# A 64-row tile with both parts side by side, and a reordered passage into the last stage

## The chip, the cores and the metric

The kernel runs on one core of one Trainium2 chip. The metric is the device time of one execution in microseconds (us). Engines are named as in the profile: PE is TensorE's matmul and PEld its weight load, DVE is VectorE, ACT is ScalarE, POOL is GpSimd, SP is the engine whose queue issues most transfers. Times in the text are counted from the start of the span.

## What is computed

Three layers follow one another, in fp32: attention with 8 global and 96 local columns, a layer of 8 experts of which each row uses one, and a channel mix with a shift by one row. The change touches the second and the third.

```python
def _moe_ref(x, w_gate, w_local, w1, w2):
    ...                                  # x: 2 x 768 rows of 512; each row has one expert e
            h = np.maximum(x[b, s] @ w1[e], 0.0)          # w1[e]: 512 x 1024
            out[b, s] = p[e] * (h @ w2[e])                # w2[e]: 1024 x 512

def _moe2_ref(x, mu_k, mu_r, w_k, w_v, w_r):
    x_prev = ...                         # x moved by one row
    xk = mu_k * x + (1.0 - mu_k) * x_prev
    xr = mu_r * x + (1.0 - mu_r) * x_prev
    k = np.maximum(xk @ w_k, 0.0)
    v = k * k @ w_v
    r = 1.0 / (1.0 + np.exp(-(xr @ w_r)))
    return (r * v).astype(np.float32)
```

## The kernel before

Each fp32 operand of a product is split into a high part (type fp32r, written by ScalarE with an activation Copy) and a low part (the difference, written by VectorE). A product is three matmuls into one PSUM bank: high by high, high by low, low by high (`mm3`, L631 to L634). Every engine works through its own queue in the order in which the program emits the instructions; inside `tc.manual_schedule()` (L1580) that order is written out by hand.

The experts are sorted by their number of rows and worked on by rank r = 0 to 7, in tiles of 128 rows. Rank 2 (`THIRD`) has a third tile of `LAST` = 64 rows. Its hidden values are split in `l1m` (L1313) into two tiles `h3h` and `h3l` of 8 chunks by 64 columns. In the second layer `l2_mm` (L659) runs 8 steps of `mm3` per tile, 512 columns wide; the stationary operand is the hidden chunk, 128 columns for a full tile and 64 for the third. `y_out` (L725) copies the bank to SBUF on ScalarE and stores it to `ys` through ScalarE's queue. Ranks 3 and 5 (`SHORT`) go through `short_expert` (L673): one tile surely, a second one under a branch (`tc.If`, L686) that this input skips. TensorE, ScalarE and VectorE all pass that branch, which stands between steps u=7 and u=8; the second turn of the tile (`turn_a(1)`) follows at u=9. Rank 7 runs two tiles through `xs_tile` (L708), 16 steps u each: 8 of the first layer, 8 of the second, turns of the hidden values in between (`hn` to `ehh`, `ehl`).

Weights are prepared ahead of use by `W_` (L1612): each call takes steps off the list `sq`. For an expert's chunk of 1024 columns these are two high halves on ScalarE and one whole low part (`w_lo_all`, L625) on VectorE; the latter also issues the next loads. For the last stage's matrices, called expert `E`, a chunk has four steps: two high halves, two low halves (for chunks 4 to 7 the second high half is on VectorE). They come in the order `WORD` = 8, 9 (w_r), 0 to 3 (w_k), 4 to 7 (w_v). `WS`, `W0` and `W7` say how many steps are taken at each step u. High and low parts live in 9 buffers each; a new chunk waits for the oldest one's last matmul. One chunk of the last stage, (E,7), instead takes two of the six `wraw` buffers that hold raw weights. The matrices of the last stage arrive as fp64 words and are decoded by three VectorE instructions per piece; `B_` (L1353) takes one such instruction at a time, and pieces are loaded through POOL's queue.

The last stage (`stage3`, L1528) works on strips b = 0 to 5 of 256 rows. A strip is gathered from `ys` by POOL, scaled by VectorE, turned by TensorE (`turn`, L1379), copied by ScalarE, mixed in two halves (`mix_a` multiplies by mu on POOL, `mix_b` adds the shifted row on VectorE), and split by `mix_hi` and `mix_lo`. Then come two `r_unit`s of 12 matmuls with a sigmoid each, eight `k_step`s of 12 matmuls of 256 columns (each followed by a ReLU and a squaring, and one step later by a split `k_split`), and two `v_unit`s of 24 matmuls. For strip 0 the r_units come ahead of the k_steps, and gathering, scaling, turning, mixing and splitting are spread by `early` over the steps u of rank 7's second tile, at the places `EARLY_AT` (u from 16 on lies in `stage3`). Strip 1 is prepared between the k_steps of strip 0, one step of the list `a` after each.

Of the kernel before, what the change touches and what calls it, by code (L numbers as in the profile page):

```python
# [16 lines left out]
P = 128  # L17
# [33 lines left out]
EARLY_AT = (7, 9, 8, 11, 12, 12, 12, 11, 12, 13, 13, 13, 13, 14, 16, 18, 16, 18)  # L51
# [517 lines left out]
def build(ctx, tc, ins, out):  # L569
# [40 lines left out]
    def w_hi1(r, c, s):  # L610
        if s == 0:
            last = (r, c) == (E, 7)
            whl[r, c] = tuple(wp.tile([P, 1024], F32R, tag="wraw" if last else f"w{x}", bufs=6 if last else 9, name=f"w{x}{r}_{c}")
                              for x in ("hi", "lo"))
# [44 lines left out]
    def l2_mm(r, ps, i, hs, m=P):  # L659
        ts_ = slice(i * P, i * P + m)  # L660
        for f in range(KF):
# [3 lines left out]
            mm3(ps[0:m, :], hh[:, ts_], hl[:, ts_], wh[:, ds_], wl[:, ds_], f == 0, f == KF - 1)  # L665
            yield f
# [58 lines left out]
    def y_out(pool, ps, row, m=P):  # L725
        yo = pool.tile([P, D], F32, tag="yo", bufs=2, name=f"yo{row}")
        nc.scalar.activation(out=yo[0:m, :], in_=ps[0:m, :], func=ACTF.Copy)  # L727
        nc.scalar.dma_start(out=ys[row:row + m, :], in_=yo[0:m, :])

# [583 lines left out]
    def l1m(r, f):  # L1313
        if r == THIRD and f == 0:
            h3["hl"] = [htile(c, f"h3{c}").rearrange("p (f c) -> p f c", f=KF) for c in "hl"]
# [15 lines left out]
        if not both:  # L1331
            relu_split(hh, hl, ps[:, 0:2 * P])
            relu_split(h3["hl"][0][:, f, :], h3["hl"][1][:, f, :], ps[:, 2 * P:N])
# [60 lines left out]
    def mix_a(b, w, a, z):  # L1394
# [5 lines left out]
        for kk in range(KD):  # L1400
            nc.gpsimd.tensor_scalar(xmix[b, w][:, kk, a:z], strips[b][:, kk, a + 1:z + 1], mu[w][:, 0, kk:kk + 1], 1.0,
                                    op0=ALU.mult, op1=ALU.mult)
# [109 lines left out]
    for u, o in zip(EARLY_AT, (("scale", 0), ("turn", 0), ("scale", 1), ("ra", 0), ("rb", 0), ("hi", 0), ("lo", 0), ("turn", 1), ("ra", 1), ("rb", 1),  # L1512
                              ("hi", 1), ("lo", 1), ("ka", 0), ("kb", 0), ("khi", 0), ("klo", 0), ("khi", 2), ("klo", 2))):
# [14 lines left out]
    def stage3():  # L1528
        small = small_words()
        for b in range(NB):  # L1530
            a, l = prep(b + 1) if b + 1 < NB else ([], [])
            if b == 0:
                gather(2)
                gather(3)
                for f in (KF + KF, KF + KF + 1):
                    early(f)
                W_(2)
                for i in range(2):
                    r_unit(b, i)
                    early(KF + KF + 2 + i)  # L1540
                    W_(5)
            for f in range(KF):
# [5 lines left out]
                if a:  # L1548
# [9 lines left out]
            k_split(b, KF - 1)  # L1558
            if b:
# [13 lines left out]
    WS = (2, 1, 2, 1, 2, 1, 2, 1) + (2, 2, 2, 2, 1, 1, 1, 1)  # L1573
# [4 lines left out]
    W7 = ((1, 0, 0, 0, 2, 1, 2, 0, 1, 2, 2, 1, 1, 0, 0, 0), (0, 0, 0, 0, 0, 2, 2, 2, 2, 0, 2, 0, 0, 0, 0, 2))  # L1578

    with tc.manual_schedule():  # L1580
# [55 lines left out]
        for r in range(1, E - 1):  # L1636
# [27 lines left out]
            for i in range(nt):  # L1664
                ps = n.bank("O", 2)
                m = nrow(r, i)
                if i == 2:
                    src, a = [tuple(h[:, f, 0:m] for h in h3["hl"]) for f in range(KF)], 0
                else:
                    src, a = [hs[r, f] for f in range(KF)], i  # L1670
                for f in l2_mm(r, ps, a, src, m):
# [245 lines left out]
```

## Time and profile before

| | us |
|---|---|
| median of 3 runs (lowest to highest) | 499.07 (498.08 to 499.48) |
| the profiled execution | 497.32 |
| its span, first to last instruction | 495.5 |
| TensorE busy in it (matmuls) | 474.6 |
| VectorE busy | 343.2 |
| ScalarE busy | 261.1 |
| POOL busy | 121.8 |

The busy time of matmuls counts pipelined instructions with modelled ends, so the distance from one start to the next says more than a duration. A row of a timeline gives the start, the time, the engine and line, the operation with the tiles that it writes and reads, and in brackets how long the engine was idle before and what ended that. All rows are of one execution.

### The profile page before, as it was taken

To read this page: it belongs to the slowest core of one execution; us is meant where nothing else is said; L and a number is where in the kernel's file an instruction comes from. 1 tells how busy PE (TensorE), PEld (TensorE's weight loads), DVE (VectorE), ACT (ScalarE), POOL (GpSimd) and SP (SyncE) were. 2 spreads that over 40 slices of the span, in tenths; PEclk is the share of its full clock that TensorE was granted. 3 is DMA by queue.
4 is the path that set the end of the run, shared out by engine and by line. 5 is a ranking of instruction groups with operands and counts; after the bars stand their busy time and mean duration, and the time that the engine had idled before them with its cause. 6 is when DMAs were issued, how large, how long until landed. Compare 5 with 4: busy or idle time off the path is not lost. (4 is left out here: it accounts for less than half of the span.)

```text
span 495.5 us, 9267 instructions
## 1 busy us (share of the span) xinstructions
PE 474.6 (96%) x3231; PEld 408.6 (82%) x3231; DVE 343.2 (69%) x889; ACT 261.1 (53%) x631; POOL 121.8 (25%) x209
## 2 busy tenths in 40 slices
PE   6999999899999999999999999999999999999994
PEld 3789888787788989768878888687989889898984
DVE  6877797796947867958878974897676948264301
ACT  4977876973326744566667655573432504243220
POOL 4111202202200000000000001825482918353220
PEclk9999999989999999999999999989999999999999
DMA  8997576784685886789699832201745533200001
GB/s 159 264 249 159 147 166 181 214 270 137 228 275 182 318 283 227 258 320 336 198 344 321 272 129 65 63 2 63 261 145 184 198 122 134 65 21 13 31 3 48
DMA packets 77128, 87.42 MB, mean 176 GB/s; under 512 B 50961, under 2 KB 51217, under 8 KB 77073
## 3 DMA queue, kind: packets, MB, share of 16 engines
q1 hardware_dynamic: 68304, 63.28, 42.0%
q0 software_dynamic: 4800, 16.78, 10.3%
q10 hardware_dynamic: 3968, 6.69, 3.6%
q8 instruction: 28, 0.46, 0.4%
q14 instruction: 28, 0.22, 0.1%
HBM read 73.75 MB, written 12.98 MB: 175 GB/s over the span
## 5 line engine op out<-in xcount | busy, mean ns | idle before, releaser
L616 ACT ACTIVATE whi<-wraw 128x512 fp32r<-128x512 f32 x128 | 72.2, 623 | 7.6 <-ACT yo L727 3.2
L625 DVE TENSOR_TENSOR wlo<-wraw,whi 128x1024 fp32r<-128x1024 f32 x55 | 66.1, 1218 | 2.1 <-ACT whi L616 2.1
L1438 ACT ACTIVATE sq<-S 128x256 f32<-128x256 f32 x48 | 18.5, 384 | 76.2 <-PE S L634 76.1
L632 PE MATMUL S<-xkh,whi 128*128 128x256 f32 x192 | 55.0, 287 | 0.7 <-ACT whi L616 0.7
L633 PE MATMUL S<-xkl,whi 128*128 128x256 f32 x192 | 53.9, 281 | 0.7 <-DVE xkl L1416 0.7
L634 PE MATMUL S<-xkh,wlo 128*128 128x256 f32 x192 | 54.0, 281 | 0.1
L1448 POOL TENSOR_TENSOR kl<-sq,kh 128x256 fp32r<-128x256 f32 x40 | 35.9, 906 | 69.6 <-issue 36.9
L1478 DVE TENSOR_TENSOR o<-O,sig 128x512 f32<-128x512 f32 (+1 forms) x13 | 8.5, 650 | 52.8 <-PE O L634 33.2
L634 PE MATMUL O<-whi,kl 128*128 128x512 f32 (+1 forms) x104 | 39.2, 377 | 0.6 <-DVE kl L1448 0.6
L633 PE MATMUL O<-wlo,kh 128*128 128x512 f32 (+1 forms) x104 | 39.0, 375 | 0.0
L632 PE MATMUL O<-whi,kh 128*128 128x512 f32 (+1 forms) x104 | 38.7, 372 | 0.0
L633 PEld LDWEIGHTS S<-xkl,whi 128*128 128x128 f32 x192 | 36.9, 192 | 1.3 <-DVE xkl L1416 1.0
L632 PEld LDWEIGHTS S<-xkh,whi 128*128 128x128 f32 x192 | 36.7, 191 | 1.3 <-ACT whi L616 0.9
L634 PEld LDWEIGHTS S<-xkh,wlo 128*128 128x128 f32 x192 | 36.7, 191 | 0.6 <-DVE wlo L621 0.6
L1439 DVE SCALAR_TENSOR_TENSOR sq<-S,sq 128x256 f32<-128x256 f32 x48 | 20.1, 420 | 15.2 <-ACT sq L1438 14.9
L277 POOL DMA_INDIRECT xs<-X,posi x12 | 13.2, 1101 | 52.9 <-DVE acc L295 19.5
L1447 ACT ACTIVATE kh<-sq 128x256 fp32r<-128x256 f32 x48 | 19.7, 412 | 12.2 <-DVE sq L1439 12.2
L634 PE MATMUL O<-whi,hl 128*128 128x512 f32 x64 | 25.1, 393 | 0.0
L633 PE MATMUL O<-wlo,hh 128*128 128x512 f32 x64 | 25.1, 392 | 0.0
L632 PE MATMUL O<-whi,hh 128*128 128x512 f32 x64 | 25.0, 391 | 0.0
L869 ACT ACTIVATE zbig<-zbig,nm 128x232 f32<-128x232 f32 (+1 forms) x48 | 22.4, 466 | 3.3 <-DVE nm L857 3.3
L634 PEld LDWEIGHTS O<-whi,kl 128*128 128x128 f32 x104 | 19.6, 188 | 4.4 <-DVE kl L1448 1.0
(433 smaller groups left out, 1418.6 us busy)
## 6 DMA issues: line engine op xcount, KB each, us to landing
wraw<-in_moe_w_dram SPq DMA_DIRECT2D x64, 512.0 KB, 5.9
dwt<-in_moe_w_v_dram POOLq DMA_DIRECT2D x8, 512.0 KB, 4.7
z<-in_moe_w_k_dram SPq DMA_DIRECT2D x8, 512.0 KB, 5.6
z<-in_moe_w_v_dram SPq DMA_DIRECT2D x8, 512.0 KB, 4.6
ys<-yo ACTq DMA_DIRECT2D x15, 256.0 KB, 5.5
xn<-xs SPq DMA_DIRECT2D x14, 256.0 KB, 4.4
vn<-in_v_dram SPq DMA_DIRECT2D x12, 256.0 KB, 4.2
dwt<-in_moe_w_k_dram POOLq DMA_DIRECT2D x6, 512.0 KB, 6.6
```

Source lines behind the costliest of these rows:

```text
L277: self.nc.gpsimd.indirect_dma_start(self.xs, bass.IndirectOffsetOnAxis(ap=self.posi[:, t:t + 1], axis=0), X[t], None)
L616: nc.scalar.activation(out=whl[r, c][0][:, sl], in_=raws[r, c][:, sl], func=ACTF.Copy)
L625: nc.vector.tensor_tensor(lo, raws.pop((r, c)), hi.bitcast(F32), op=ALU.subtract)
L632: nc.tensor.matmul(out_, lhsT=ah, rhs=bh, start=first, stop=False)
L633: nc.tensor.matmul(out_, lhsT=ah, rhs=bl, start=False, stop=False)
L634: nc.tensor.matmul(out_, lhsT=al, rhs=bh, start=False, stop=last)
L869: nc.scalar.activation(out=pe, in_=pe, func=ACTF.Exp, scale=-1.0, bias=nm[:, h:h + 1], accum_out=sm[:, h:h + 1])
L1438: nc.scalar.activation(out=sq_, in_=ps[:, 0:TB], func=ACTF.Relu)
L1439: nc.vector.scalar_tensor_tensor(sq_, ps[:, 0:TB], 0.0, sq_, op0=ALU.max, op1=ALU.mult)
L1447: nc.scalar.activation(out=hh, in_=sq_, func=ACTF.Copy)
L1448: (nc.gpsimd if b else nc.vector).tensor_tensor(hl, sq_, hh.bitcast(F32), op=ALU.subtract)
L1478: nc.vector.tensor_tensor(o[:, a:z], ps[:, 0:z - a], sig[b, i][:, a:z], op=ALU.mult)
```

## The change

- The third tile of rank 2: high and low hidden values stand side by side, 64 and 64 columns, in two tiles of four chunks (`h3["t"]`). `l2_both` runs two matmuls per chunk, with the high and the low weights, so that the bank's rows 0 to 63 hold the products of the high parts and rows 64 to 127 those of the low parts. `y_both` copies rows 64 to 127 on ScalarE, adds rows 0 to 63 on VectorE and stores through POOL's queue. The product of the two low parts is now included.
- No word is decoded in that tile; in rank 7 words are decoded only at u = 11 to 15 of the first tile.
- (E,9) instead of (E,7) takes the `wraw` buffers; `W7` splits (E,9) in the first tile of rank 7, and `stage3` takes 2 + 3 + 3 steps ahead of the k_steps instead of 2 + 5 + 5.
- One step of `WS` moves from u=6 to u=12.
- Strip 0's `mix_a` runs on ScalarE (activation Copy with a column as scale); `EARLY_AT` ends at u=15, and the second turn and the k mix come earlier in the order.
- A sigmoid of 8 values ahead of rank 7.
- In strip 0 the last step of the list `a` (`mix_b` of strip 1's r) comes after the last `k_split`.

```diff
--- before.py
+++ after.py
@@ -48,7 +48,7 @@
 NTAB = (5, 4)
 X1_AT = (5, 7)
 WNEXT = (1,) * 12 + (0,) * 4
-EARLY_AT = (7, 9, 8, 11, 12, 12, 12, 11, 12, 13, 13, 13, 13, 14, 16, 18, 16, 18)
+EARLY_AT = (7, 9, 9, 10, 10, 11, 11, 11, 12, 12, 12, 13, 13, 13, 15, 15, 15, 15)
 
 
 class Net:
@@ -609,7 +609,7 @@
 
     def w_hi1(r, c, s):
         if s == 0:
-            last = (r, c) == (E, 7)
+            last = (r, c) == (E, WORD[1])
             whl[r, c] = tuple(wp.tile([P, 1024], F32R, tag="wraw" if last else f"w{x}", bufs=6 if last else 9, name=f"w{x}{r}_{c}")
                               for x in ("hi", "lo"))
         sl = slice(s * 512, s * 512 + 512)
@@ -663,6 +663,14 @@
             ds_ = slice((f % 2) * 512, (f % 2) * 512 + 512)
             hh, hl = hs[f]
             mm3(ps[0:m, :], hh[:, ts_], hl[:, ts_], wh[:, ds_], wl[:, ds_], f == 0, f == KF - 1)
+            yield f
+
+    def l2_both(r, ps, ts_):
+        for f in range(KF):
+            ds_ = slice((f % 2) * 512, (f % 2) * 512 + 512)
+            for j, w in enumerate(whl[r, 4 + f // 2]):
+                nc.tensor.matmul(ps, lhsT=ts_[f // 4][:, f % 4].rearrange("p s c -> p (s c)"), rhs=w[:, ds_],
+                                 start=f + j == 0, stop=f == KF - 1 and j == 1)
             yield f
 
     TB = 2 * P
@@ -726,6 +734,12 @@
         yo = pool.tile([P, D], F32, tag="yo", bufs=2, name=f"yo{row}")
         nc.scalar.activation(out=yo[0:m, :], in_=ps[0:m, :], func=ACTF.Copy)
         nc.scalar.dma_start(out=ys[row:row + m, :], in_=yo[0:m, :])
+
+    def y_both(pool, ps, row, m):
+        yo = pool.tile([P, D], F32, tag="yo", bufs=2, name=f"yo{row}")
+        nc.scalar.activation(out=yo[0:m, :], in_=ps[m:2 * m, :], func=ACTF.Copy)
+        nc.vector.tensor_tensor(yo[0:m, :], ps[0:m, :], yo[0:m, :], op=ALU.add)
+        nc.gpsimd.dma_start(out=ys[row:row + m, :], in_=yo[0:m, :])
 
     zp0 = wstack.enter_context(tc.tile_pool(name="zp0", bufs=1))
     w3 = {nm: ins[nm].bitcast(U32) for nm in ("w_k", "w_v", "w_r")}
@@ -1312,7 +1326,7 @@
 
     def l1m(r, f):
         if r == THIRD and f == 0:
-            h3["hl"] = [htile(c, f"h3{c}").rearrange("p (f c) -> p f c", f=KF) for c in "hl"]
+            h3["t"] = [htile(c, f"h3{c}").rearrange("p (f s c) -> p f s c", f=KF // 2, s=2) for c in "hl"]
         N = xhl[r][0].shape[2]
         both = N <= 2 * P
         odd = f % 2
@@ -1330,7 +1344,8 @@
         hs[r, f] = (hh, hl)
         if not both:
             relu_split(hh, hl, ps[:, 0:2 * P])
-            relu_split(h3["hl"][0][:, f, :], h3["hl"][1][:, f, :], ps[:, 2 * P:N])
+            t3 = h3["t"][f // 4][:, f % 4]
+            relu_split(t3[:, 0, :], t3[:, 1, :], ps[:, 2 * P:N])
         elif odd:
             relu_split(*pair["h"], pair["ps"])
 
@@ -1398,8 +1413,11 @@
             else:
                 xmix[b, w] = zp0.tile([P, KD, TB], F32, tag="z0", bufs=2, name=f"xm{w}{b}")
         for kk in range(KD):
-            nc.gpsimd.tensor_scalar(xmix[b, w][:, kk, a:z], strips[b][:, kk, a + 1:z + 1], mu[w][:, 0, kk:kk + 1], 1.0,
-                                    op0=ALU.mult, op1=ALU.mult)
+            o, x, m = xmix[b, w][:, kk, a:z], strips[b][:, kk, a + 1:z + 1], mu[w][:, 0, kk:kk + 1]
+            if b:
+                nc.gpsimd.tensor_scalar(o, x, m, 1.0, op0=ALU.mult, op1=ALU.mult)
+            else:
+                nc.scalar.activation(out=o, in_=x, func=ACTF.Copy, scale=m)
 
     def mix_b(b, w, a, z):
         for kk in range(KD):
@@ -1509,8 +1527,8 @@
                 mix_lo(0, "k", 0, TB, i, i + 2)
 
     EARLY = {}
-    for u, o in zip(EARLY_AT, (("scale", 0), ("turn", 0), ("scale", 1), ("ra", 0), ("rb", 0), ("hi", 0), ("lo", 0), ("turn", 1), ("ra", 1), ("rb", 1),
-                              ("hi", 1), ("lo", 1), ("ka", 0), ("kb", 0), ("khi", 0), ("klo", 0), ("khi", 2), ("klo", 2))):
+    for u, o in zip(EARLY_AT, (("scale", 0), ("turn", 0), ("scale", 1), ("ra", 0), ("rb", 0), ("turn", 1), ("hi", 0), ("lo", 0), ("ra", 1), ("rb", 1),
+                              ("ka", 0), ("hi", 1), ("lo", 1), ("kb", 0), ("khi", 0), ("klo", 0), ("khi", 2), ("klo", 2))):
         EARLY.setdefault(u, []).append(o)
 
     def small_words():
@@ -1532,20 +1550,17 @@
             if b == 0:
                 gather(2)
                 gather(3)
-                for f in (KF + KF, KF + KF + 1):
-                    early(f)
                 W_(2)
                 for i in range(2):
                     r_unit(b, i)
-                    early(KF + KF + 2 + i)
-                    W_(5)
+                    W_(3)
             for f in range(KF):
                 if f in (1, 2) and a:
                     scale(2 * b + 1 + f)
                 k_step(b, f)
                 if f:
                     k_split(b, f - 1)
-                if a:
+                if a and (b or f < KF - 1):
                     a.pop(0)()
                 if b == 0:
                     W_(2)
@@ -1556,6 +1571,8 @@
                 elif b == 4 and f == 6:
                     n.small_w3(rp)
             k_split(b, KF - 1)
+            if b == 0:
+                a.pop(0)()
             if b:
                 for i in range(2):
                     r_unit(b, i)
@@ -1570,12 +1587,12 @@
                 s()
 
     DVEHI = (4, 5, 6, 7)
-    WS = (2, 1, 2, 1, 2, 1, 2, 1) + (2, 2, 2, 2, 1, 1, 1, 1)
+    WS = (2, 1, 2, 1, 2, 1, 1, 1) + (2, 2, 2, 2, 2, 1, 1, 1)
     BL = {1: ((0, 0, 0, 0, 1, 0, 1, 0), 4), 2: ((1, 1, 1, 0, 1, 1, 1, 0), 3), 6: ((1, 1, 1, 0, 1, 1, 1, 0), 2)}
     LATE = 4
     W0 = (0,) * 8 + (2, 2, 2, 2, 1, 1, 1, 1)
     B0 = (0, 0, 0, 0, 0, 0, 0, 1, 1, 0, 0, 1, 1, 1, 1, 0)
-    W7 = ((1, 0, 0, 0, 2, 1, 2, 0, 1, 2, 2, 1, 1, 0, 0, 0), (0, 0, 0, 0, 0, 2, 2, 2, 2, 0, 2, 0, 0, 0, 0, 2))
+    W7 = ((1, 0, 0, 0, 2, 1, 2, 0, 1, 2, 2, 1, 1, 2, 0, 2), (0, 0, 0, 0, 0, 2, 2, 2, 2, 0, 0, 0, 0, 0, 0, 0))
 
     with tc.manual_schedule():
         lq = []
@@ -1664,23 +1681,24 @@
             for i in range(nt):
                 ps = n.bank("O", 2)
                 m = nrow(r, i)
-                if i == 2:
-                    src, a = [tuple(h[:, f, 0:m] for h in h3["hl"]) for f in range(KF)], 0
-                else:
-                    src, a = [hs[r, f] for f in range(KF)], i
-                for f in l2_mm(r, ps, a, src, m):
+                steps = l2_both(r, ps, h3["t"]) if i == 2 else l2_mm(r, ps, i, [hs[r, f] for f in range(KF)])
+                for f in steps:
                     if f == 0 and i == 0:
                         W_(2)
                     elif f < (7, 4, 0)[i]:
                         W_(1)
                     if r == LATE:
                         next(late, None)
-                    elif f % BL[r][1] == BL[r][1] // 2:
+                    elif i < 2 and f % BL[r][1] == BL[r][1] // 2:
                         B_(1)
-                y_out(rp, ps, BASES[r] + TILES[r][i] * P, m)
+                if i == 2:
+                    y_both(rp, ps, BASES[r] + TILES[r][i] * P, m)
+                else:
+                    y_out(rp, ps, BASES[r] + TILES[r][i] * P)
 
         for _ in late:
             pass
+        nc.scalar.activation(out=rp.tile([1, 8], F32, name="sg1"), in_=n.ones[0:1, 0:8], func=ACTF.Sigmoid)
         r = E - 1
         for i in range(2):
             hn = wp.tile([P, 2, D], F32, tag="wraw", bufs=6, name=f"hn{i}")
@@ -1690,7 +1708,7 @@
                 if i:
                     early(u)
                 W_(W7[i][u])
-                B_(1)
+                B_(u > 10)
             if i == 0:
                 for _ in bg:
                     pass
```

## Rows read from the trace of the kernel before

**Rows 1.** Windows: us, each engine's busy time (instructions), granted clock, DMA share, GB/s.

```profile
324.00:325.00 1.00, 1.00 (x5) 0.92 (x5) 1.00 (x4) 1.00 (x4) 0.00 (x0) 0.50 0.00 0
...
350.00:360.00 10.00, 10.00 (x90) 9.96 (x89) 7.22 (x17) 5.17 (x14) 6.60 (x8) 1.00 0.97 337
```

**Rows 2.** TensorE's timeline at the third tile: start, duration, line, operation.

```profile
207.65 0.39 PE L632 MATMUL O<-whi,h3h 128*64 128x512 f32 x1
...
213.13 0.39 PE L632 MATMUL S<-whi,xh 128*128 128x512 f32 x1
```

**Rows 3.** TensorE's timeline in the short experts; brackets: idle before, what ended it.

```profile
221.90 0.63 PE L642 MATMUL PT<-ident,ha3l 128*128 128x128 f32 x4 [0.85 <-DVEq L686]
...
259.82 0.63 PE L642 MATMUL PT<-ident,ha5l 128*128 128x128 f32 x4 [0.71 <-DVEq L686]
```

**Rows 4.** VectorE's timeline in the short expert of rank 3.

```profile
219.34 2.35 DVE L625 TENSOR_TENSOR wlo<-wraw,whi 128x1024 fp32r<-128x1024 f32 x2
```

**Rows 5.** TensorE's timeline from rank 7's second tile to the first v_units.

```profile
311.52 0.50 PE L634 MATMUL O<-whi,ehl 128*128 128x512 f32 x1 [0.41 <-DVE ehl L646]
...
313.93 0.39 PE L632 MATMUL PT<-whi,xrh 128*128 128x512 f32 x1
...
320.03 0.28 PE L632 MATMUL S<-xkh,whi 128*128 128x256 f32 x1
321.03 0.39 PE L633 MATMUL S<-xkl,whi 128*128 128x256 f32 x1 [0.73 <-DVE xkl L1416]
...
323.36 0.54 PE L632 MATMUL S<-xkh,whi 128*128 128x256 f32 x1 [0.74 <-ACT whi L616]
...
334.68 0.28 PE L632 MATMUL S<-xkh,whi 128*128 128x256 f32 x1
...
336.04 0.39 PE L632 MATMUL O<-whi,kh 128*128 128x512 f32 x1
...
342.07 0.51 PE L634 MATMUL O<-whi,kl 128*128 128x512 f32 x1 [0.59 <-DVE kl L1448]
342.41 0.40 PE L632 MATMUL O<-whi,kh 128*128 128x512 f32 x1
```

**Rows 6.** Chain that ended last: start, length, engine, tile, line.

```profile
328.49 0.44 PE R L1385 x4
```

**Rows 7.** POOL's timeline while strip 0 is mixed.

```profile
309.56 4.14 POOL L1401 TENSOR_SCALAR xmr<-strip,mur 128x128 f32<-128x128 f32 x8 [2.89 <-ACT strip L1386]
313.69 2.36 POOL L1401 TENSOR_SCALAR xmk<-strip,muk 128x256 f32<-128x256 f32 x4
```

**Rows 8.** VectorE's timeline in the passage into the last stage.

```profile
309.17 0.48 DVE L1367 TENSOR_SCALAR yg<-yg,PEX 128x512 f32<-128x512 f32 x1 [1.06 <-DMA yg<-ys,yposi]
...
310.77 0.69 DVE L646 TENSOR_TENSOR ehl<-PT,ehh 128x512 fp32r<-128x512 f32 x1
...
326.08 0.42 DVE L1439 SCALAR_TENSOR_TENSOR sq<-S,sq 128x256 f32<-128x256 f32 x1
...
331.52 1.28 DVE L621 TENSOR_TENSOR wlo<-z,whi 128x512 fp32r<-128x512 f32 x2
...
333.39 0.42 DVE L1606 CAST whi<-z 128x512 fp32r<-128x512 f32 x1
...
340.01 1.66 DVE L1406 SCALAR_TENSOR_TENSOR zbig<-zbig,mur 128x256 f32<-128x256 f32 x4
341.60 0.41 DVE L1448 TENSOR_TENSOR kl<-sq,kh 128x256 fp32r<-128x256 f32 x1
```

**Rows 9.** ScalarE's timeline at rank 7's first tile and at the first sigmoid.

```profile
291.46 0.60 ACT L656 ACTIVATE hn<-S 128x512 f32<-128x512 f32 x1 [1.06 <-DVE z L487]
...
320.89 1.28 ACT L1462 ACT_TABLE_LOAD   x1
```

**Rows 10.** ScalarE's groups by line and shape: count, busy, mean ns, idle before.

```profile
L869 ACT ACTIVATE zbig<-zbig,nm 128x232 f32<-128x232 f32 x40 | 19.2, 480 | 2.3 <-DVE nm L857 2.3
...
L869 ACT ACTIVATE zbig<-zbig,nm 128x128 f32<-128x128 f32 x8 | 3.2, 395 | 1.0 <-DVE nm L857 1.0
```

## The prediction, made before the kernel had run

> **What bounds the kernel.** I read the windows of the span first. From 343 us to the end TensorE has no idle time: the stretch 350 to 360 has it busy for 10.00 of 10.00 us at full granted clock, while VectorE works 7.22 and ScalarE 5.17 [rows 1]. So whatever makes TensorE reach 343 us earlier moves the end by as much, unless it is taken back on the way. The list of who waited for whom and TensorE's timeline then show where the time before 343 us can be had. First, matmuls that can be left out: the third tile of the expert of rank 2 streams without a gap from 207.65 to 213.13, and the next expert's first matmul follows at once [rows 2]. Second, two waits in the two short experts, 0.85 and 0.71 us, both ended by VectorE's branch [rows 3]. Third, the passage into the last stage: waits of 0.41, 0.73, 0.74 and 0.59 us and a stretch at 324 us in which the granted clock is 0.50, the 1.2 GHz level [rows 1, 5]. TensorE had been interrupted from 320 to 324 before that fall.
>
> **The third tile.** Before, 8 steps of 3 matmuls make 24, which take 213.13 - 207.65 = 5.48 us, or 0.228 each [rows 2]. After, the stationary operand holds 64 high and 64 low columns, so 2 matmuls per step do it: 16, and 8 x 0.228 = 1.83 us go. A matmul with 128 stationary columns has the same duration as one with 64, 0.39 [rows 2, 5], so I cost the wider one at nothing. Added are a VectorE addition (nearest row: a two-operand 128x512 with PSUM, 0.69 [rows 8]) and a store on POOL's queue instead of ScalarE's. Neither is waited for by TensorE: the bank is one of two and the rows are gathered only in the last stage. Behind the addition on VectorE stand low parts of the next expert; three decode instructions leave VectorE there, so its queue gets shorter. Cost nothing; without that cover 0.69.
>
> **The short experts.** TensorE's turn of the second half waits for VectorE to pass the branch [rows 3]. In the expert before that branch VectorE has two low parts of 1.18 each one behind the other, ending at 221.69 [rows 4]; the wait ends 0.2 later. The new WS moves one W_ step from u=6 to u=12, so the twelfth step, the second of these low parts, falls behind the branch. VectorE passes 1.18 earlier, more than either wait. ScalarE keeps its two high parts ahead of the branch. I take both waits as gone, 0.85 + 0.71 = 1.56; bounds 0 (ScalarE's own branch then ends the wait) and 1.56.
>
> **Moved words and the table.** The last four decode instructions now run at the end of the first tile of rank 7, where VectorE is next wanted by the second tile; they feed the last pair of matrix parts, split some 30 us later. Nothing. The table load of 1.28 [rows 9] leaves the place where the first sigmoid, and a weight part behind it, are waited for. It now lies ahead of the ReLU at 291.46, before which ScalarE was idle 1.06 [rows 9]. Load and tiny sigmoid make it at most half a microsecond late, and TensorE turns its result two accumulation steps (6 x 0.228 = 1.37) after it could start. Nothing; bound 0.5. The Trainium skill (ScalarE: Activation LUTs, What ACT_TABLE_LOAD costs) gives about 2.66 us for a change of set, a drain included. The row's 1.28 is followed by the sigmoid itself, so no drain shows here; by the page's figure the ReLU would be some 1.9 late and TensorE would lose about 1.1.
>
> **The passage into the last stage.** Its order, by the times of before:
> - Rank 7's second tile ends at 313.93 as before. The 0.41 wait for ehl [rows 5] goes, since VectorE now does the two scalings around it: but scaling 1 now comes behind a pair of low parts (1.28, the nearest pair) and ehl (0.69) instead of at 309.17 when its gather lands [rows 8], so it is done at about 310.4, and the second turn, due at 310.05, waits 0.4 in its place. Sum 0, between +0.4 and -0.4.
> - Mixing: POOL's 8 instructions of 128x128 take 4.14 and then 4 of 128x256 take 2.36, in one chain until 316.05 [rows 7]. On ScalarE the nearest rows are its activations with a column operand, 0.395 for 128x128 and 0.480 for 128x232 [rows 10]; successive ones overlap by some 0.1 (an estimate), which makes about 0.3 and 0.4 start to start. So 1.2 for the first four, 1.2 for the next four, 1.6 for the last. Strip 1 is copied at 311.5, the first high part is done at 312.1, its low part at 312.9, a microsecond before the first r_unit wants it. Mixes end at 314.9, the second low part at 316.1, before the second r_unit (316.7). Then four VectorE mixes of 0.4 and the two halves of the k operand, until 319.1; the first k_step wants them at 319.4.
> - So the two r_units take 24 x 0.228 = 5.48 rather than 320.03 - 313.93 = 6.10 [rows 5].
> - The first k_step needs matrix parts 0 to 3. Before, three chunks were split here; now (E,9) is split a tile earlier, in buffers that held raw weights already used, so two remain, behind the k operand on ScalarE. Two high parts, a sigmoid and another high part end near 320.5, its low part at 321.2: a wait of up to 1.0 for the last quarter of the first k_step. Before, this step took two waits of 0.73 and 0.74 and half clock [rows 1, 5].
> - Undisturbed, a k_step is 336.04 - 334.68 = 1.36 and a turn 0.44 [rows 5, 6]. Eight and two make 11.8; before they took 336.04 - 320.03 = 16.0.
> - The v_unit is 5.48 without a wait; before, 6.37 to 342.41 [rows 5].
>
> TensorE alone gives 313.9 + 5.5 + 1.0 + 11.8 + 5.5 = 337.7 for the end of that v_unit; without the 1.0 it is 336.7. VectorE gives the other bound: from its first squaring (326.08) to its last low part (342.01) it is busy nearly throughout [rows 8]. It now carries a chunk more (1.28 + 0.42) and one mix of strip 1 less (1.66, moved behind the last low part), so 15.9 again. Starting at 322.2, it ends at 338.1, and the v_unit's last step 0.4 later, 338.5. I take 337.7, with VectorE idle 0.5 less than before: gain 342.41 - 337.7 = 4.7, bounds 3.9 and 5.7. Gathers 2 and 3 are no longer behind the mixes on POOL; they only get earlier.
>
> **Sum.** 1.83 + 1.56 + 4.7 = 8.1. The profiled execution took 497.32 with a span of 495.5, so it would take 489.2. The median of the three runs shown is 499.07 (498.08 to 499.48), 1.75 above that one; from it the forecast is 491.0.
>
> **A rule against the change.** ScalarE's 0.395 for 128x128 stands on an activation with a column operand [rows 10]. The Trainium skill (ScalarE: Activation LUTs, What ACT_TABLE_LOAD costs) says that such an operand adds some 93 ns; an estimate from the page is 0.386, so the trace agrees, and the scale here is such an operand. Had each mix been as cheap as without one, the chain of 12 would be 1.1 shorter and the 1.0 wait would go.
>
> **Rivals.**
> - B, the passage starves again. VectorE or ScalarE fall behind in the k_steps, TensorE is interrupted and the clock falls to 1.2 GHz as at 324. For it: the first k_step's slack is 0.3 and VectorE has no idle time in this stretch. Against it: the waits left sum to 1.4, not 2.6. It costs a step and a half at half clock (1.4) and further waits of 1.5: 491.0 + 2.9 = 493.9.
> - C, the gains ahead of 300 us are taken back, since ScalarE's branch ends the wait instead and weights arrive at their old pace. For it: all conversions are in one queue order with the turned halves. Against it: in the list of waits no weight part holds TensorE from rank 1 to rank 7. Then 499.07 - 4.7 = 494.4.
> - D, slower. ScalarE, in order, becomes the chain: the 12 mixes hold back high parts, E2 and E3 behind them. Each 0.1 us more per mix delays the first k_step by 1.2. It decides where a mix costs 0.7 more than 0.3 to 0.4, over 1.0 each, which uses up all 8.1; at 1.2 it gives about 501. The rows at 0.395 and 0.480 speak against it.
> - E, it does not do what it says: the buffers for (E,9) are not free, and its high part blocks ScalarE ahead of the first tile's store, on which the gathers depend. Each microsecond of that is a microsecond at the end; 3 us of it would give 494.0. The raw weights of rank 7 are split before that point, so I hold it unlikely.
>
> **How the numbers follow.** My forecast has 0.66, B 0.17, C 0.08, E 0.03, D 0.03, and 0.03 is for gains that cancel. About 0.3% (1.5 us) is what a measurement of this kernel can tell from no change. That makes 0.93 faster, 0.04 within, 0.03 slower. The forecast's own bounds are 491.0 - 1.0 (passage at 5.7) and 491.0 + 2.4 (passage at 3.9 and both branch waits left). The range adds about 1 us below for the spread of the runs and takes in B and C above: 489.0 to 495.0.
>
> **What would show it.** In the profile after: 16 matmuls between the second tile and rank 3's first matmul, 3.7 us; no wait on VectorE's branch over 0.1; no work of POOL on strip 0's mixing, and ScalarE's mixes near 0.39 and 0.5; the r_units 5.5 apart from the first k_step; no stretch at half clock at the first k_step; the first v_unit's end 24 us after the second tile's end instead of 28.5. A half-clock stretch there, or a wait of TensorE on a mixed strip, makes the forecast wrong by B or D.

## The result, and the profile after

Four runs of the changed kernel had a median of 492.83 us (491.19 to 493.79), beside 498.57 (497.83 to 499.48) of the kernel before: ratio 0.9858, 95% interval 0.9818 to 0.9898. A second measurement gave 491.57 against 499.07, ratio 0.9868 (0.9832 to 0.9904). The profiled execution took 491.19 with a span of 489.2; before, 497.32 and 495.5. So the change saves some 6 to 7 us (6.6 and 7.1 by the two ratios, 5.7 and 7.5 by the two pairs of medians), and its time lies in the forecast range, 1.8 above the forecast itself.

The windows of the changed kernel, for the places of [rows 1] (columns as there):

```profile
320.00:325.00 5.00, 5.00 (x46) 5.00 (x46) 4.80 (x13) 3.47 (x9) 0.62 (x1) 1.00 0.02 5
350.00:360.00 10.00, 10.00 (x58) 8.66 (x57) 9.54 (x18) 4.36 (x10) 9.84 (x14) 1.00 0.55 191
```

The half-clock stretch at 324 us is gone: from the first r_unit to the second v_unit the granted clock reads 1.00. TensorE is without idle time from 320 to 325. In the second window VectorE now works 9.54 of 10.00.

TensorE's timeline of the changed kernel at the third tile and in the short experts, which answers to [rows 2, 3]:

```profile
207.68 0.39 PE L672 MATMUL O<-whi,h3h 128*128 128x512 f32 x1
...
211.34 0.39 PE L632 MATMUL S<-whi,xh 128*128 128x512 f32 x1
...
219.08 0.60 PE L642 MATMUL PT<-ident,ha3l 128*128 128x128 f32 x4
...
256.35 0.60 PE L642 MATMUL PT<-ident,ha5l 128*128 128x128 f32 x4
```

The 16 matmuls take 3.66 instead of 5.48, and neither turn has a bracket for idle time any more. Its timeline in the passage, which answers to [rows 5]:

```profile
305.02 0.66 PE L1400 MATMUL R<-ident,yg 128*128 128x128 f32 x4 [0.20 <-DVE yg L1382]
307.21 0.66 PE L1400 MATMUL T<-ident,yg 128*128 128x128 f32 x4 [0.16 <-DVE yg L1382]
...
310.47 0.39 PE L632 MATMUL PT<-whi,xrh 128*128 128x512 f32 x1
...
315.96 0.28 PE L632 MATMUL S<-xkh,whi 128*128 128x256 f32 x1
...
328.99 0.40 PE L632 MATMUL O<-whi,kh 128*128 128x512 f32 x1
...
333.19 0.39 PE L632 MATMUL O<-whi,kh 128*128 128x512 f32 x1
333.94 0.51 PE L633 MATMUL O<-wlo,kh 128*128 128x512 f32 x1 [0.35 <-DVE wlo L621]
...
335.21 0.39 PE L632 MATMUL O<-whi,kh 128*128 128x512 f32 x1
```

Start by start against before, TensorE is ahead by 1.79 at rank 3's first matmul (211.34 for 213.13), 2.82 at rank 3's turn, 3.47 at rank 5's, 3.46 at the r_units, 4.07 at the first k_step and 7.20 at the second v_unit (335.21 for 342.41). At the end it is ahead by 6.3 (the spans). The two waits of the first k_step that are left are 0.21 for a high part and 0.23 for a low part.

### The profile page after: what moved, and what is told of

The parts are those of the page before. It is cut to its first block, busy times and chain, and to the rows that moved or that the text cites. A ratio compares the mean times of both kernels' runs of the same rounds, so it can differ in the third digit from the quotient of the medians.

```text
span 489.2 us, 9260 instructions
## 1 busy us (share of the span) xinstructions
PE 471.5 (96%) x3223; PEld 408.7 (84%) x3223; DVE 343.0 (70%) x890; ACT 265.1 (54%) x644; POOL 113.4 (23%) x198
## 5 line engine op out<-in xcount | busy, mean ns | idle before, releaser
L633 PEld LDWEIGHTS O<-wlo,kh 128*128 128x128 f32 x104 | 19.6, 188 | 4.6 <-DVE wlo L621 0.8
```

Of the source, the lines that this page charges most:

```text
L633: nc.tensor.matmul(out_, lhsT=ah, rhs=bl, start=False, stop=False)
```

## The experiments

The expectations stand as they were written before each run. The ratios are to the kernel before, run on the same chip:

| kernel | median | ratio (95% interval) |
|---|---|---|
| third tile's form alone | 500.76 | 1.0038 (1.0006 to 1.0071) |
| third tile, words off it | 496.74 | 0.9949 (0.9925 to 0.9974) |
| WS alone | 497.94 | 0.9973 (0.9947 to 0.9998) |
| passage alone | 495.48 | 0.9929 (0.9893 to 0.9964) |
| changed, passage undone | 494.41 | 0.9900 (0.9867 to 0.9933) |
| changed, strip 0 mixed on POOL | 493.10 | 0.9880 (0.9837 to 0.9923) |
| changed, words back | 494.35 | 0.9923 (0.9893 to 0.9953) |
| changed, no early sigmoid | 492.91 | 0.9898 (0.9872 to 0.9924) |
| changed, (E,7) for (E,9) | 494.48 | 0.9924 (0.9900 to 0.9948) |
| changed, last mixing step early | 495.53 | 0.9945 (0.9923 to 0.9967) |
| changed, w_v's halves on ScalarE | 491.36 | 0.9844 (0.9811 to 0.9876) |
| changed, again | 491.57 | 0.9868 (0.9832 to 0.9904) |

The intervals are 2.4 to 4.3 us wide, so differences of a microsecond are read from the traces. These compare places inside a span, since the attention layer, which no experiment touches, differed by up to 2.3 us from one profiled execution to the next.

### The third tile alone, and with the words off it

The first kernel is the one before with the third tile's new form (`l2_both`, `y_both`, the two tiles of four chunks) and nothing else.

> The kernel before with the third tile's new form alone (two matmuls per chunk, copy on ScalarE, addition on VectorE, store through POOL's queue). Theory 1, the three parts add up: rank 3's first matmul 1.83 us earlier, 24 matmuls become 16, and nothing else moves, so the time falls by 1.8 us. Theory 2, gains ahead of the last stage are taken back there: the 1.8 us are seen at rank 3 and less than 0.9 of them is left at the first v_unit.

It is slower than before: 500.76, ratio 1.0038 with an interval above 1. Rank 3's first matmul comes 1.66 earlier (1.82 when both are counted from the third tile's first matmul), as it should, and then more than that is lost. VectorE's timeline, first of the kernel before, then of this one:

```profile
209.81 0.69 DVE L489 SCALAR_TENSOR_TENSOR z<-dwt,z 128x512 uint32<-128x512 uint32 x1
214.15 0.43 DVE L485 TENSOR_SCALAR z<-dwt 128x512 uint32<-128x512 uint32 x1 [3.64 <-DMA dwt<-in_moe_w_v_dram]
...
218.73 0.69 DVE L646 TENSOR_TENSOR ehl<-PT,ehh 128x512 fp32r<-128x512 f32 x1 [0.43 <-ACT ehh L644]
```

```profile
215.52 0.43 DVE L485 TENSOR_SCALAR z<-dwt 128x512 uint32<-128x512 uint32 x1 [4.86 <-DMA dwt<-in_moe_w_v_dram]
217.32 0.68 DVE L741 TENSOR_TENSOR yo<-O,yo 64x512 f32<-64x512 f32 x1
217.92 2.34 DVE L625 TENSOR_TENSOR wlo<-wraw,whi 128x1024 fp32r<-128x1024 f32 x2
220.19 0.68 DVE L646 TENSOR_TENSOR ehl<-PT,ehh 128x512 fp32r<-128x512 f32 x1
```

In both, a decode instruction inside the third tile waits for its words to arrive, 3.64 and 4.86. Before, the low part `ehl` behind it came in time: it waited for its own high part. Here the longer wait, the addition and a TensorE that wants `ehl` 1.7 earlier use that cover up. TensorE's waits of this kernel, and its windows with the granted clock in the third column from the end:

```profile
220.92 0.71 PE L634 MATMUL O<-whi,ehl 128*128 128x512 f32 x1 [2.47 <-DVE ehl L646]
223.33 1.09 PE L642 MATMUL PT<-ident,ha3l 128*128 128x128 f32 x4 [0.43 <-DVEq L694]
```

```profile
221.00:224.00 3.00, 2.57 (x8) 1.69 (x8) 2.13 (x2) 0.00 (x0) 0.00 (x0) 0.51 0.86 315
224.00:227.00 3.00, 3.00 (x18) 2.63 (x18) 1.91 (x3) 2.52 (x5) 0.00 (x0) 0.93 1.01 377
```

A wait of 2.47 is followed by some 3 us at 0.51, the 1.2 GHz level. The second kernel has the same form and the words moved as in the change:

```diff
-                    elif f % BL[r][1] == BL[r][1] // 2:
+                    elif i < 2 and f % BL[r][1] == BL[r][1] // 2:
...
-                B_(1)
+                B_(u > 10)
```

> The kernel before with the third tile's two matmuls per step and the words taken off that tile (decoded at u = 11 to 15 in rank 7 and at the end of its first tile); WS and the passage as before. Theory 1 (the words are what made the third tile alone slower): no wait for words in the third tile, rank 3's first matmul and its turn 1.8 earlier than before, no half clock there, 496.5 to 497.5, ratio 0.995 to 0.997. Theory 2 (something else in the third tile's form, as the store on POOL's queue or the addition on VectorE, cost those 4 us): no faster than before, and waits on a low part early in rank 3 as in the third tile alone.

496.74, ratio 0.9949: 2.5 saved (1.3 to 3.7). In and behind the third tile no instruction of VectorE waits for words; its addition stands at 213.79, and `ehl` waits for ScalarE as before:

```profile
213.79 0.69 DVE L741 TENSOR_TENSOR yo<-O,yo 64x512 f32<-64x512 f32 x1 [1.64 <-ACT yo L740]
...
218.36 0.69 DVE L646 TENSOR_TENSOR ehl<-PT,ehh 128x512 fp32r<-128x512 f32 x1 [1.17 <-ACT ehh L644]
```

Rank 3's first matmul, set against the 1.68 by which this execution was late at the end of the attention layer, is 1.84 early. The third kernel of this group is the changed one with the two lines above put back.

> The changed kernel with only the words put back where they were: one decode instruction every second or third step of the third tile too, and in rank 7 one at every step as long as there are any. Theory 1 (taking the words off the third tile is what makes its gain last; learnt from the run of the third tile alone, in which VectorE's addition stood behind a decode that waited 4.86 us for its words): VectorE waits over 4 us for words inside the third tile, TensorE waits some 2 to 3 us for a low part early in rank 3 and falls to half clock there, and rank 3's turn loses 3 to 5 us against the changed kernel: about 495 to 497. Theory 2 (my prediction's step, which costed that move at nothing): within 0.5 of the changed kernel, 493.

494.35, ratio 0.9923. In its profile VectorE waits 5.27 for words in the third tile, TensorE 2.88 for `ehl`, and the clock is 0.50 from 222 to 228. VectorE's row, TensorE's row and the window:

```profile
217.49 0.43 DVE L485 TENSOR_SCALAR z<-dwt 128x512 uint32<-128x512 uint32 x1 [5.27 <-DMA dwt<-in_moe_w_v_dram]
```

```profile
222.89 0.80 PE L634 MATMUL O<-whi,ehl 128*128 128x512 f32 x1 [2.88 <-DVE ehl L646]
```

```profile
222.00:228.00 6.00, 5.11 (x17) 4.23 (x18) 4.03 (x6) 1.71 (x3) 0.00 (x0) 0.50 0.87 286
```

TensorE leaves that stretch 5.8 later than the changed kernel's. This execution is the slowest of the six (492.06 to 498.69), and the median is only some 3 above what the changed kernel's ratio would give on this chip; whether the wait for words differs that much between executions is open. The mechanism of theory 1 stands in all three kernels, and by the median its price is at the lower end of the 3 to 5 expected.

### WS alone

```diff
-    WS = (2, 1, 2, 1, 2, 1, 2, 1) + (2, 2, 2, 2, 1, 1, 1, 1)
+    WS = (2, 1, 2, 1, 2, 1, 1, 1) + (2, 2, 2, 2, 2, 1, 1, 1)
```

> The kernel before with the one moved step of WS alone. Theory 1: the two waits for VectorE's branch (0.85 and 0.71) vanish and the time falls by 1.6 to 1.9 us. Theory 2: VectorE's branch was late only because of the words decoded in the third tile, which stay here; then the wait in rank 3 stays near 0.85 and only that of rank 5 goes, 0.7 us in all.

497.94, ratio 0.9973: 1.3 saved, with an interval of 0.1 to 2.6. In the trace the turn of rank 3 comes 0.61 earlier and that of rank 5 1.46 earlier than in [rows 3], both without a bracket. This execution was already 0.33 late at rank 3's first matmul (213.46 for 213.13); counted from there the gains are 0.94 and 1.79, as theory 1 has it:

```profile
221.29 0.63 PE L642 MATMUL PT<-ident,ha3l 128*128 128x128 f32 x4
...
258.36 0.60 PE L642 MATMUL PT<-ident,ha5l 128*128 128x128 f32 x4
```

### The passage as a whole

First the changed kernel with the passage undone: strip 0 mixed on POOL, the old order and places, (E,7) in the buffers of raw weights, no early sigmoid, the last mixing step early. Third tile, words and WS stay changed.

> The changed kernel with its passage into the last stage undone: mixing of strip 0 on POOL, old order and places of the early steps, (E,7) in the raw buffers, no early sigmoid, mix_b of strip 1 ahead of the last split. Theory 1: third tile and branch waits keep their 3.6 us and the passage's 3.7 are lost, so it lies about 3.6 us under the kernel before and some 2.5 to 3.7 above the changed one, with the first v_unit's end 3.5 us earlier than before. Theory 2: the passage was bound by the gathers, and an earlier arrival lengthens its waits; then its end is earlier by less than 2.

494.41, ratio 0.9900, about 2 slower than the changed kernel by the ratios, whose intervals overlap. In its trace the passage, from the first r_unit to the second v_unit, takes 28.07 (311.42 to 339.49), for 28.48 before and 24.74 in the changed kernel. Then the other way round, the kernel before with the passage alone.

> The kernel before with the passage into the last stage alone (mixing of strip 0 on ScalarE, its order and places, (E,9) in the buffers of the raw weights, early sigmoid, last mixing step of strip 1 moved); third tile, words and WS as before. Theory 1 (my prediction's term of 4.7 for the passage is a gain by itself): 4 to 5 below the kernel before, 0.99, and no half clock at the first k_step. Theory 2 (the changed kernel with the passage undone lost only about 2 us against the changed kernel, so the parts share what they save): 2 to 3 below, 0.995.

495.48, ratio 0.9929: 3.5 saved (1.8 to 5.3). The three parts by themselves save 2.5, 1.3 and 3.5, together 7.3; all at once 6 to 7. Within intervals this wide they add up, which does not rule out that they share a microsecond or two. The passage alone has no half clock at the first k_step (1.00 in each window from 316 to 330), as its theory 1 has it, but by the times its size lies between the two theories: both kernels put it between 2 and 5. The trace is sharper. TensorE's first r_unit and second v_unit of the passage alone:

```profile
315.88 0.39 PE L632 MATMUL PT<-whi,xrh 128*128 128x512 f32 x1
...
340.64 0.39 PE L632 MATMUL O<-whi,kh 128*128 128x512 f32 x1
```

They are 24.76 apart, as in the changed kernel (24.74), so in that stretch the passage saves its 3.7 with or without the other parts.

With the passage undone the starving comes back only in part. TensorE's waits of the changed kernel with the passage undone, and its windows:

```profile
318.53 0.39 PE L633 MATMUL S<-xkl,whi 128*128 128x256 f32 x1 [0.72 <-DVE xkl L1431]
...
320.85 0.39 PE L632 MATMUL S<-xkh,whi 128*128 128x256 f32 x1 [0.73 <-ACT whi L616]
...
324.05 0.39 PE L632 MATMUL S<-xkh,whi 128*128 128x256 f32 x1 [0.72 <-DVE sq L1454]
```

```profile
320.00:322.00 2.00, 1.04 (x6) 0.72 (x6) 1.45 (x3) 2.00 (x5) 0.33 (x1) 1.00 0.00 0
322.00:324.00 2.00, 1.33 (x12) 1.14 (x10) 2.00 (x6) 1.50 (x4) 0.00 (x0) 1.00 0.00 0
324.00:326.00 2.00, 1.95 (x17) 1.95 (x18) 2.00 (x6) 0.68 (x2) 0.00 (x0) 1.00 0.00 0
```

The first two waits are those of before [rows 5], but here the clock stays at 1.00.

### The passage, piece by piece

Which engine mixes: the changed kernel with the branch in `mix_a` removed, so that strip 0 is mixed on POOL at the new places.

> The changed kernel with strip 0 mixed on POOL again, everything else as changed, its order too. Theory 1, the mixing engine is what the passage gained by: POOL needs 4.1 + 2.4 us in one chain and VectorE mixes more slowly beside it (2.0 instead of 1.1 for four); the k operand is ready 1.5 to 2 us later and so is the first v_unit. Theory 2, the earlier places and the earlier split of (E,9) did it: the k operand is late by 0.5 us or less, and as ScalarE is free of 4 us of mixing the first v_unit moves by less than 0.5 either way.

493.10, ratio 0.9880. In the trace TensorE takes 18.74 from the first r_unit to the first v_unit; the changed kernel's two profiles have 18.52 and 18.32. The first k_step has two waits, 0.33 and 0.23. POOL's mixing costs a few tenths once the order is the new one, as theory 2 has it. VectorE's own second four mixes of strip 0 take 0.45 to 0.56 each beside POOL's here, and 0.34 each in the changed kernel.

The table load: the changed kernel without the line of the early sigmoid.

> The changed kernel without the early sigmoid of 8 values, so that the table load of 1.28 us falls again at the first sigmoid of strip 0, between two high parts of w_k on ScalarE. Theory 1: the high and low parts behind it come 1.28 later, TensorE waits 1.0 to 1.3 more in the first k_step, and the end is later by as much: 494. Theory 2: the first k_step has its parts early enough (it waited only 0.21 and 0.23 in the changed kernel), so that at most 0.4 is lost: 493.

492.91, ratio 0.9898. Medians alone don't settle it (the interval overlaps the changed kernel's), but the trace does for this execution, the slowest of the five. ScalarE's timeline, then TensorE's waits and windows:

```profile
318.61 1.28 ACT L1480 ACT_TABLE_LOAD   x1
319.91 0.60 ACT L1480 ACTIVATE sig<-PT 128x512 f32<-128x512 f32 x1
320.40 0.62 ACT L616 ACTIVATE whi<-zbig 128x512 fp32r<-128x512 f32 x1
```

```profile
321.07 0.38 PE L632 MATMUL S<-xkh,whi 128*128 128x256 f32 x1 [1.65 <-ACT whi L616]
...
321.80 0.39 PE L634 MATMUL S<-xkh,wlo 128*128 128x256 f32 x1 [0.23 <-DVE wlo L621]
```

```profile
323.00:325.00 2.00, 2.00 (x12) 2.00 (x11) 1.07 (x4) 0.80 (x3) 0.00 (x0) 0.50 0.00 0
```

The load makes the high part behind it late, TensorE waits 1.65 instead of 0.21, and half clock follows: against the changed kernel 1.4 by the wait and 1.5 by the clock. Theory 1 stands for the wait; the half clock neither theory had.

The second chunk: `last` is (E,7) and `W7` and the steps ahead of the k_steps are the old ones; order and ScalarE's mixes stay new.

> The changed kernel with (E,7) instead of (E,9) in the buffers of the raw weights, and the old split order of rank 7 and of the last stage (three chunks of w_k between the second tile and the first k_step instead of two). ScalarE mixes and the order of the mixing stay as changed. Theory 1: the 0.9 to 1.3 of high parts per chunk on ScalarE and 1.2 of low parts on VectorE come back into the passage, TensorE waits 1.5 to 2.5 more ahead of or in the first k_step, half clock comes back there: 495. Theory 2 (the order of mixing alone filled the passage): within 0.5 of the changed kernel.

494.48, ratio 0.9924. Four waits of 0.41, 0.58, 0.58 and 0.71 stand between 318 and 323, three of them for low parts of w_k, one for a squaring behind them on VectorE. The clock stays at 1.00. From the r_units to the second v_unit TensorE takes about 2 more. Theory 1 in the waits, not in the clock.

The last mixing step of strip 1: `a.pop(0)()` back ahead of the last split.

```diff
-                if a and (b or f < KF - 1):
+                if a:
                     a.pop(0)()
...
-            if b == 0:
-                a.pop(0)()
```

> The changed kernel with the last mixing step of strip 1 (four VectorE instructions, 1.66 us together) back ahead of the last split of strip 0. Theory 1: the last low part comes 1.66 later, and the first v_unit of strip 0, which waits for it (0.35 for an earlier one in the changed kernel), is held up by 1 to 1.7 at its end: 494.2. Theory 2: the last low part is wanted only by the v_unit's last step, 5 us after its start, and has the slack: within 0.4 of the changed kernel.

495.53, ratio 0.9945, the dearest of the pieces. TensorE's timeline of this kernel:

```profile
334.89 0.39 PE L632 MATMUL O<-whi,kh 128*128 128x512 f32 x1
337.28 0.50 PE L633 MATMUL O<-wlo,kh 128*128 128x512 f32 x1 [2.00 <-DVE wlo L621]
...
337.96 0.63 PE L632 MATMUL O<-whi,kh 128*128 128x512 f32 x1
...
340.95 0.48 PE L633 MATMUL O<-wlo,kh 128*128 128x512 f32 x1
```

The wait is 2.00, for 0.35 and 0.64 in the changed kernel's two profiles. Counted from the first r_unit, the matmul that waits starts after 25.23 (337.28 - 312.05), for 23.47 in both of those: 1.76 later, where four mixes of 1.66 now stand ahead of the low part. Then seven matmuls are 0.427 apart ((340.95 - 337.96) / 7) instead of 0.229, another 1.4. A low part that came 1.76 later cost some 3.

### VectorE's bound

The changed kernel with the second high halves of w_v on ScalarE.

```diff
-    DVEHI = (4, 5, 6, 7)
+    DVEHI = ()
```

> The changed kernel with the second high halves of the last four chunks (w_v) on ScalarE, as those of w_k already are, instead of on VectorE. In the changed kernel VectorE gives the bound of the k_steps of strip 0: it does these four in 0.42 to 0.53 each, and the only wait left there is 0.35 for a low part at the first v_unit. Theory 1 (VectorE is the bound): its low parts come up to 1.8 earlier, the 0.35 goes, end earlier by 0.3 to 0.5: 492.4. Theory 2: ScalarE now does two high halves in a row (1.13) where ReLU and the high part of the hidden values wait behind them, so that the k_steps wait instead: slower by 0.5 to 1.5.

491.36, ratio 0.9844, against 491.57 and 0.9868 of the changed kernel on the same chip. The times can't tell them apart. In the trace the first v_unit's low part comes earlier: the matmul that waits for it starts 23.15 after the first r_unit (334.28 - 311.13), for 23.47 in both profiles of the changed kernel (333.94 - 310.47 and 334.75 - 311.28), and no wait of TensorE on ScalarE takes its place:

```profile
333.77 0.39 PE L632 MATMUL O<-whi,kh 128*128 128x512 f32 x1
334.28 0.50 PE L633 MATMUL O<-wlo,kh 128*128 128x512 f32 x1
```

So VectorE was the bound there, by 0.3, the lower end of what theory 1 expected. It is the only variant that isn't behind the changed kernel.

### The changed kernel again

> The changed kernel once more, unchanged. In its first profile TensorE's steps of 512 columns are 0.234 instead of 0.229 apart in some stretches of the last stage, though no wait stands there and the granted clock reads 1.00; together they cost about 1 us of the 7.2 that the passage gained. Theory 1 (these stretches belong to an execution, not to the instructions): here they lie at other places or are shorter, and span less their excess is the same. Theory 2 (they belong to the changed order): they stand at the same places, near 225, 323 to 334, 341 to 349 and 405 to 421. In both: 492.8 against 498.6, 1.0 to 1.2% below the kernel before.

491.57, ratio 0.9868. In this profile TensorE is ahead of before by 3.38 at rank 5's turn, 2.65 at the r_units, 6.39 at the second v_unit and 6.3 at the end: the passage saves the same 3.74, and where the first profile lost 0.9 behind the passage, this one loses 0.7 ahead of it. The last section uses its trace.

## Why the prediction came out as it did

**Third tile: right, with the wrong reason for its cover.** 1.83 was forecast and 1.79 came; the wider stationary operand cost nothing. The step that failed is "three decode instructions leave VectorE there, so its queue gets shorter", costed at nothing, with 0.69 as the price without cover. What stood there wasn't work but a wait, 3.64 for words in the trace of before, and the price of leaving the words in place is the whole gain and more: 2.88 of waiting and a stretch at half clock. Moving the words isn't a by-product of the new tile; it is what lets it gain. The sum was safe only because the change does both. The row stands in the trace of before, and the prediction made no use of it.

**Short experts: right.** 1.56 forecast. Both waits on the branch are gone, and after the third tile's 1.79 TensorE gains 1.03 and 0.65 up to the second turn, 1.68. WS alone: 1.79 in its trace, counted from rank 3's first matmul, and 1.3 by the times.

**Moved words and table: right where they went, under-told where they left.** In rank 7 neither a decode nor the load of 1.28 at 286.21 holds TensorE. But the load's old place would have cost a wait of 1.65 in the new passage. The Trainium skill (ScalarE: Activation LUTs, What ACT_TABLE_LOAD costs) gives about 2.66 us for a change of set, drain included; the load without the early sigmoid took 1.28 with the sigmoid 0.02 behind it (318.61 + 1.28 to 319.91), so no drain shows after it, and the measurement decides.

**Passage: the mechanism right, 4.7 forecast and 3.74 measured.** From the r_units to the second v_unit TensorE took 28.48 before and 24.74 after; I had 23.8. Term by term:
- The scaling's waits 0.20 and 0.16 for a forecast 0.4; the r_units 5.49 for 5.48.
- ScalarE's twelve mixes: 1.28 and 1.27 for four of 128x128 and 1.70 for four of 128x256, their starts 0.30 and 0.40 apart, for 0.3 and 0.4.
- The k_steps, waits included: 13.03 for 12.8. The wait of up to 1.0 was 0.21 + 0.23.
- The first v_unit: 6.22 for 5.48. This is the term that failed. I had two bounds and took TensorE's (337.7) over VectorE's (338.5). VectorE's held: I gave it 15.9 from its first squaring to its last low part.

VectorE's timeline of the changed kernel, at both ends of that stretch:

```profile
318.98 0.42 DVE L1457 SCALAR_TENSOR_TENSOR sq<-S,sq 128x256 f32<-128x256 f32 x1
...
333.20 1.28 DVE L621 TENSOR_TENSOR wlo<-z,whi 128x512 fp32r<-128x512 f32 x2
334.41 0.41 DVE L1466 TENSOR_TENSOR kl<-sq,kh 128x256 fp32r<-128x256 f32 x1
```

From 318.98 to 334.82 are 15.84. With VectorE's bound the sum would have been 8.1 - 0.8 = 7.3, against 7.20 measured at that place. The other runs bear it out: in the second profile TensorE's k_steps were 0.2 shorter (12.83) and its wait for the low part 0.3 longer, so the waiting matmul started after 23.47 as before; it moved when VectorE's work changed, to 23.15 with w_v's halves on ScalarE and to 25.23 with the last mixing step early.

**What made the passage better.** I gave the mixes on ScalarE as much room as the rest; once the order is the new one they are worth 0.2 to 0.4. The chunk split ahead of time, the table load and the place of one mixing step cost 2 to 3 each in the traces when one alone is put back, 8 together, where the whole passage gains 3.74 and, undone as a whole, loses 3.3. Pieces of a tight passage don't add up: the load of 1.28 put back alone shows as 1.44 more of waiting, the mixes of 1.66 as a low part 1.76 later, and in two of the three cases half clock follows.

**Rivals.** B, a starving passage, didn't happen in the changed kernel, but its mechanism and price did as soon as one piece was taken out: a wait, then half clock, 3 in the kernel with the last mixing step early (I had 2.9). C, gains ahead of 300 taken back, didn't in the first profile: 3.47 at rank 5 is 3.46 at the r_units. In the second 0.7 is lost there, but by no engine that TensorE waits for (last section). D fell with mixes 0.30 and 0.40 apart. E fell too: VectorE's and ScalarE's passages show no wait for those buffers.

**After 335 us** I had expected nothing, and in the first profile 0.9 of the 7.20 is given back though TensorE waits for nothing: the last section. In the second profile nothing is (6.39, then 6.3), so this loss belongs to the execution. Of the forecast's 8.1 for the profiled execution 6.13 came (497.32 - 491.19): about 1 is missing in the passage, and about 0.9 behind it.

## What to carry to other kernels

Before work is added to an in-order queue, or its reader made earlier, look for a wait inside that queue nearby (a bracket on a transfer): such a wait is free only while the reader is later still. Where two engines bound a stretch closely, take the later bound, from the engine that is busy throughout, and count its instructions one by one. On a TensorE that is otherwise full, a single late operand can cost twice its wait: behind the attention layer, in each profile here in which TensorE waited 1.65 us or more at once, half clock followed. It cost 1.4 to 1.5 more without the early sigmoid and with the last mixing step early, and 2.9 with the words back, where it lasted over 6 us.

## What the runs showed of the hardware

**When half clock follows.** In the fourteen profiles, behind the attention layer, half clock followed a single wait of 1.65 (no early sigmoid), 2.00, 2.47 and 2.88, each time within 2 us. No other single wait there is longer than 0.85. It didn't follow four waits of 0.41 to 0.71 within 5 us ((E,7) for (E,9)). The pair 0.73 and 0.74 of before [rows 5] was followed by it, and so was the same pair in the three other kernels that kept the old passage: the third tile's form alone (0.72 and 0.74; clock 0.50 from 327 to 330), WS alone (0.73 and 0.73; 0.50 from 322 to 325) and the third tile with the words off it (0.72 and 0.74; 0.51 from 324 to 326). But it did not follow the pair 0.72 and 0.73 with the passage undone. What separates these stays open.

**Matmuls 4 ns further apart, at full clock.** In some stretches that hold from one group of turns to the next, matmuls of 256 columns are 0.1175 apart instead of 0.1135, and those of 512 columns 0.2333 instead of 0.2288: some 4 ns each whatever the columns, so it isn't a clock ratio, and the granted clock reads 1.00. The changed kernel's two profiles show r_units of the same strip in both ways, six matmuls from the first line to the second; first profile, then second:

```profile
413.30 0.40 PE L633 MATMUL PT<-wlo,xrh 128*128 128x512 f32 x1
...
414.70 0.40 PE L633 MATMUL PT<-wlo,xrh 128*128 128x512 f32 x1
```

```profile
413.28 0.39 PE L634 MATMUL PT<-whi,xrl 128*128 128x512 f32 x1
...
414.65 0.39 PE L634 MATMUL PT<-whi,xrl 128*128 128x512 f32 x1
```

1.40 against 1.37. In the first the wide stretches of the last stage lie at 323 to 352 and 405 to 438, in the second at 437 to 455 and 477 to 482; before, at 444 to 462. The same instructions do both, so in the last stage the execution decides, as the repeat's theory 1 has it. In the second profile a wide stretch also runs from 259 to 291, ahead of the passage, and its excess of 0.7 is what that execution lost between rank 5's turn and the r_units. One between 221 and 239, of 54 matmuls or more, is in all eleven profiles with the new third tile and in none of the three with the old one, so it does go with the instructions. Summed over the steps of three matmuls that were more than 2.5 ns wide for each matmul, the excess after 340 us is some 1.1 in the changed kernel and 0.5 before, 0.6 of the 0.9 lost there. Over whole spans it is some 1 to 3 in the fourteen profiles. With it taken off, the spans of the changed kernel's two profiles are equal to 0.1 (487.0 each) and that of the variant with w_v's halves on ScalarE is some 0.5 lower (486.5). What sets a stretch into this state wasn't tried.
